# Three partition sums as pairs of fp32r products, with one sum and one denominator moved, in an adaLN block

## The chip, the cores and the metric

The kernel runs on one core of a Trainium2 chip. The metric is the device time of one execution in microseconds, as the median of several runs.

## The reference

A block with adaptive layer norm: linear attention, then a bilinear gated feed-forward layer. The input x has 2048 tokens of 512 numbers, there are 32 heads of 16, and the feed-forward layer is 1376 wide. Everything is fp32.

```python
mod = (silu(c) @ w_mod).reshape(1, 6, 1, 512)
sa, ca, ga, sb, cb, gb = the six rows of mod
h = layernorm(x) * (1 + ca) + sa
q, k, v = heads of h @ wqkv
pq, pk = phi(q), phi(k)            # phi(t) = (t + 1 where t > 0, else exp(t)) + 1e-6
kv = einsum("bhsd,bhse->bhde", pk, v)
z = einsum("bhsd->bhd", pk)        # sum of phi(k) over all tokens
num = einsum("bhqd,bhde->bhqe", pq, kv)
den = einsum("bhqd,bhd->bhq", pq, z)[..., None] + 1e-6
x = x + ga * ((num / den) @ wo)
h = layernorm(x) * (1 + cb) + sb
out = x + gb * (((h @ w_gate) * (h @ w_up)) @ w_down)
```

## The kernel before

The order of all instructions is written out by hand: each engine runs its queue in the order of the code, and waits only for the data it needs. Tiles have 128 partitions and mostly 512 columns. The tokens are 16 tiles in 4 chunks; SBUF tiles come from one pool of 99 buffers, PSUM banks from two pools of four (`acc_bank`, `bank`).

Products are made from split operands: `split` (L182 to L184) copies a tile to fp32r on ScalarE (the high part h, L183) and subtracts it from the original on VectorE, or on another engine named by `low` (the low part l, L184). `product` (L192 to L198) then adds three fp32r products for each pair of tiles: high by high, high by low, low by high.

Sums over the 128 partitions are not split before the change. Row v of mod is gathered in an accumulator tile by `mod_acc` (L156 to L161, VectorE: each w_mod tile times silu(c), added). For the rows that are needed as columns, `mod_col` (L163) multiplies the accumulator by one column of `ones`. For rows 2 (ga) and 5 (gb) `mod_row` (L174 to L179) multiplies a 128x128 tile of ones by the accumulator in one fp32 product of 512 columns (L176), so that each partition holds the sum, and ScalarE copies it out (L178). The sum z of phi(k) is treated likewise: `z_add` (L304) adds the tiles on VectorE into `zacc`, one fp32 product sums over the partitions (L512), and ScalarE writes `zb` (L514).

The main loop (L458 to L517) runs over the 16 tiles i. In tile i TensorE makes the k or q product for two tiles ahead (`proj`, L196 to L198) and adds tile i into the four accumulators of x-hat by phi(k) (`t_tile`, L323 to L325). ScalarE and VectorE make phi (L287, L288, L291), and the dictionary `extra` (L443) hangs the loading and gathering of mod, and the splitting of wo, on tiles 4 to 15. In tile 14 stand the last gathering step of row 5 (L161) and the four splits of wo; in tile 15 the sum of z, `t_tile`, and then row 5's sum.

Behind the loop, VectorE makes `den_z` (L528, L529), which needs zb, and the denominators of the first chunk: `den_a` for a tile is a product with zb (L534) and a sum over each head (L540). ScalarE scales the four accumulators by ca (L583), VectorE adds zb times sa (L584), and both split the four results into `tt` (L183, L184). TensorE has `proj(6)` and `proj(7)` in the meantime, and then the key-value product `kvps` (L592 to L594): 48 products of 128 columns, from wv and `tt`. VectorE then takes the diagonal blocks of it (L601), `w_out` multiplies them into wo and by ga (L571), and the attention output, the second norm and the feed-forward layer follow, with gb scaling w_down (L706, L1043).

Of the kernel before, what the change touches and what calls it, by code (L numbers as in the profile page):

```python
# [9 lines left out]
F32R = mybir.dt.float32r  # L10
# [4 lines left out]
P = 128  # L15
# [7 lines left out]
def tile_adaln_block(  # L23
# [12 lines left out]
    nc = tc.nc  # L36
# [23 lines left out]
    consts = pool("consts", 1)  # L60
# [10 lines left out]
    def T(p, tag, shape=(P, D), dt=F32, bufs=None):  # L71
        cnt[0] += 1
        return p.tile(list(shape), dt, tag="t" if p is tiles else tag, name=f"{tag}_{cnt[0]}", bufs=bufs)

    def B(tag, shape=(P, D), dt=F32):

        return T(tiles, tag, shape, dt)
# [4 lines left out]
    def bank():  # L82
        return T(ps_w, "bank")
# [6 lines left out]
    ones = consts.tile([P, P], F32, name="ones")  # L90
# [17 lines left out]
    def load(src, tag):  # L108
        raw = B(tag, (P, *src.shape[1:]))[:src.shape[0]]
        nc.sync.dma_start(raw, src)  # L110
        return raw
# [4 lines left out]
    def load_mod(v):  # L116
        return [load(wm_v[:, k, v * D:(v + 1) * D], "raw") for k in range(KD)]
# [38 lines left out]
    def mod_acc(acc, raws, ks):  # L156
        for k in ks:
            if k == 0:
                nc.vector.tensor_scalar(acc, raws[k], sc[:, 0:1], None, op0=ALU.mult)
            else:  # L160
                nc.vector.scalar_tensor_tensor(acc, raws[k], sc[:, k:k + 1], acc, op0=ALU.mult, op1=ALU.add)  # L161

    def mod_col(acc, ps):  # L163

        for b in range(KD):
            nc.tensor.matmul(ps[:, b:b + 1], acc[:, b * P:(b + 1) * P], ones[:, 0:1], start=True, stop=True)
        return ps

    def col_out(v, ps, add):
        t = consts.tile([P, KD], F32, name=f"col{v}")  # L170
        nc.vector.tensor_scalar(t, ps[:, :KD], add, None, op0=ALU.add)
        return t

    def mod_row(v, acc):  # L174
        ps = bank()
        nc.tensor.matmul(ps, ones, acc, start=True, stop=True)  # L176
        t = consts.tile([P, D], F32, name=f"row{v}")
        nc.scalar.activation(t, ps, AF.Copy)  # L178
        return t  # L179


    def split(src, h, l, low=None):  # L182
        nc.scalar.activation(h, src, AF.Copy)  # L183
        (low or nc.vector).tensor_tensor(l, src, f32(h), op=ALU.subtract)  # L184

    def split_raw(raw, shape=(P, D), low=None):
        h = B("w", shape, F32R)
        l = B("w", shape, F32R)
        split(raw, h[:raw.shape[0]], l[:raw.shape[0]], low)
        return h, l  # L190
# [82 lines left out]
    NT = NCH * NJ  # L273
# [4 lines left out]
    def proj(i, w, of=bank):  # L278

        ch, j = divmod(i, NJ)  # L280
        ps = of()
        product(ps, [(cut(norm[ch].t[k], j * P, (j + 1) * P), w[k]) for k in range(KD)])
        return ps
# [9 lines left out]
    def k_split_x(i):  # L293
        ch, j = divmod(i, NJ)
        kx[i] = [B("xh", dt=F32R), B("xl", dt=F32R)]
        split(norm[ch].n[j], *kx[i])

    def k_phi(i, ps):
        phi = B("phi")
        phi_a(ps, phi)  # L300
        phi_b(ps, phi)
        phk[i] = phi

    def z_add(i):  # L304
        if i == 1:
            nc.vector.tensor_tensor(zacc, phk[0], phk[1], op=ALU.add)
        elif i > 1:
            nc.vector.tensor_tensor(zacc, zacc, phk[i], op=ALU.add)
        phk.pop(i - 1, None)

    def k_split(i):
        h, l = B("kh", dt=F32R), B("kl", dt=F32R)
        phi = phk[i]
        nc.scalar.activation(h, phi, AF.Identity, bias=eps_phi)
        nc.vector.scalar_tensor_tensor(l, phi, EPS_PHI, f32(h), op0=ALU.add, op1=ALU.subtract)
        kx[i] += [h, l]

    def t_tile(i, *ks):
        xh, xl, kh, kl = kx[i]
        first, last = i == 0, i == NT - 1  # L320
        for k in ks:
            a, b = k * P, (k + 1) * P
            nc.tensor.matmul(tacc[k], xh[:, a:b], kh, start=first, stop=False)  # L323
            nc.tensor.matmul(tacc[k], xl[:, a:b], kh, start=False, stop=False)  # L324
            nc.tensor.matmul(tacc[k], xh[:, a:b], kl, start=False, stop=last)  # L325

    def q_a(i, ps):
        phq[i] = B("h")
        q_ps[i] = ps
        phi_a(ps, phq[i])  # L330

    def q_b(i):
        phi_b(q_ps.pop(i), phq[i])

    zacc = B("z")
# [94 lines left out]
    rows, cols = {}, {}  # L430
    accs = {}

    raw_m, raw_o, wo_s = {}, [], []

    def mod_load(*vs):
        raw_m.update({v: load_mod(v) for v in vs})

    def mod_part(v, *ks):
        if 0 in ks:
            accs[v] = B("f")  # L440
        mod_acc(accs[v], raw_m[v], ks)
# [4 lines left out]
             7: lambda: (wv.extend(split_raw(r) for r in raw_v[3:4]),),  # L446
             8: lambda: (mod_part(2, 0, 1), mod_load(3)),
             9: lambda: (mod_part(2, 2, 3), mod_load(4)),
             10: lambda: (mod_part(3, 0, 1, 2), mod_load(5)),
             11: lambda: (mod_part(3, 3), mod_part(4, 0, 1), rows.update({2: mod_row(2, accs[2])})),  # L450
             12: lambda: (raw_o.extend(load(wo_v[k], "raw") for k in range(KD)), mod_part(4, 2, 3), cols.update({3: col_out(3, mod_col(accs[3], bank()), 0.0)})),
             13: lambda: (mod_part(5, 0, 1, 2), cols.update({4: col_out(4, mod_col(accs[4], bank()), 1.0)})),
             14: lambda: (mod_part(5, 3), wo_s.extend(split_raw(x) for x in raw_o)), 15: lambda: rows.update({5: mod_row(5, accs[5])})}
    q_at = {3: 0, 4: 1, 6: 2, 7: 3}
    ahead = {2: k_ps[2], 3: k_ps[3]}
    turn_at = {4 * ch + j: (ch + 1, 2 * j, 2 * j + 1) for ch in range(1, NCH - 1) for j in range(2)}
    turn_at.update({1: (1, 0, 1), 2: (1, 2, 3)})
    for i in range(NT):  # L458
        ch, j = divmod(i, NJ)
        done = 0  # L460
        if i > 2:
            ahead[i + 2] = proj(i + 2, wk) if i + 2 < NT else proj(i + 6 - NT, wq)
        if i in q_at:
            qps = proj(q_at[i], wq)
        def turn_x():
            to, *ks = turn_at[i]
            nx.transpose(*ks)
            nx.modulated(ca, sa, *ks, cast=nc.vector)
            norm[to:] = [nx]

        fresh = i > 0 and ch + 1 < NCH and j == 0
        if i == 2:
            turn_x()
            wq.extend(split_raw(r) for r in raw_q)
        if fresh:
            nx.xhat(2)
        if 0 < i < NT - 1:
            k_split_x(i + 1)
        if fresh:
            nx.xhat(3)  # L480
        if 0 < i < NT - 1:
            k_split(i + 1)
        if i in turn_at and i != 2:
            t_tile(i, 0, 1)
            done = 2
            turn_x()
        if i == 2:
            t_tile(i, *range(KD))
            done = KD
            ahead[i + 2] = proj(i + 2, wk)  # L490
        if ch + 2 < NCH and j == 2:
            nx2 = Norm(xts[ch + 2])
            nx2.stats(0, 1)
        if ch + 2 < NCH and j == 3:
            nx = nx2
            nx.stats(2, 3)
            nx.rstd_of()
            nx.nmr_of()
            nx.xhat(0, 1)
        if i + 2 < NT:  # L500
            k_phi(i + 2, ahead.pop(i + 2))
        else:
            q_a(i + 6 - NT, ahead.pop(i + 2))
            q_b(i + 6 - NT)
        if i in q_at:
            q_a(q_at[i], qps)
            q_b(q_at[i])
        if i + 1 < NT:
            z_add(i + 1)
        if i == NT - 1:  # L510
            zps = bank()
            nc.tensor.matmul(zps, ones, zacc, start=True, stop=True)  # L512
            zb = consts.tile([P, D], F32, name="zb")
            nc.scalar.activation(zb, zps, AF.Identity, bias=eps_z)  # L514
        t_tile(i, *range(done, KD))
        if i in extra:
            extra[i]()  # L517
    ga, gb, sb, cb = rows[2], rows[5], cols[3], cols[4]


    dens = {}
# [4 lines left out]
    def den_z():  # L526

        nc.vector.reduce_sum(den0, zb.rearrange("p (h i) -> p h i", i=DH), axis=AX.X)  # L528
        nc.vector.tensor_scalar(den0, den0, EPS_PHI, EPS_DEN, op0=ALU.mult, op1=ALU.add)  # L529

    def den_p(ch, *js, on=None):
        for j in js:
            pzs[ch, j] = B("f")
            (on or nc.gpsimd).tensor_tensor(pzs[ch, j], phq[ch * NJ + j], zb, op=ALU.mult)  # L534
# [7 lines left out]
    def den_a(ch, *js, on=None):  # L542

        for j in js:
            den_p(ch, j, on=on)
            den_r(ch, j)
# [13 lines left out]
    def q_tile(i):  # L560
        q_a(i, proj(i, wq))
# [13 lines left out]
            split(f, *wp[-1])  # L575

    den_z()
    den_a(0, 0, 1, on=nc.vector)
    ps = proj(6, wq)
    fs, tt = [], []  # L580
    for k in range(KD):
# [6 lines left out]
        split(f, *tt[-1])  # L588
    q_a(6, ps)
    q_tile(7)  # L590
    kvps = bank()
    for g in range(KD):  # L592
        a, b = g * P, (g + 1) * P
        product(kvps[:, a:b], [(cut(wv[k], a, b), cut(tt[k], a, b)) for k in range(KD)])  # L594
    q_b(6)
    q_b(7)
    den_a(0, 2, on=nc.vector)
    ps = proj(8, wq)
    kvp = (B("xh", dt=F32R), B("xl", dt=F32R))
    kvf = B("n")  # L600
# [7 lines left out]
    ps = proj(9, wq)  # L608
# [470 lines left out]
    ps = proj(11, wq)  # L1079
# [185 lines left out]
```

## Time and profile before

| | |
|---|---|
| median of 3 runs | 566.05 us (565.7 to 566.51) |
| the profiled execution | 565.84 us, its span 564.1 us |
| granted TensorE clock | 0.999 |
| TensorE busy | 556.8 us (99% of the span) |
| VectorE busy | 377.4 us (67%) |
| ScalarE busy | 278.5 us (49%) |
| GpSimd busy | 187.0 us (33%) |

The span is the time from the first to the last instruction in the profile; the execution's own time is 1.7 us longer. In the rows, PE is TensorE, PEld its weight loads, DVE VectorE, ACT ScalarE, POOL GpSimd and SP the queue that issues the DMAs. A row of the timeline gives the start, the time from the start of the first to the end of the last of a few like instructions, engine, line, operation, output and inputs, shapes, and how many they are; in brackets stands how long the engine was idle before, and what released it. Starts of an engine's neighbouring instructions lie closer together than their durations, because the end of one overlaps the start of the next.

### The profile page before, as it was taken

What the parts mean: (1) busy time and instruction counts of PE and PEld (TensorE: products, weight loads), DVE (VectorE), ACT (ScalarE), POOL (GpSimd) and SP (SyncE); (2) the same over time, 40 slices, a digit from 0 to 9 for tenths busy, and PEclk for the clock granted to TensorE, in tenths of its full rate; (3) what the DMA queues carried; (4) which work ended last, traced back from release to release, by engine and by line L of the source; (5) the groups of instructions that cost most, each with busy time, mean ns of one, the idle gap of its engine ahead of it and who ended that gap; (6) DMA issues with size and microseconds to landing.
All of it is one profiled execution on the core that took longest, in us unless ns stands there. A gap on an engine that the chain in (4) does not pass through costs nothing.

```text
span 564.1 us, 7356 instructions
## 1 busy us (share of the span) xinstructions
PE 556.8 (99%) x2568; PEld 457.1 (81%) x2568; DVE 377.4 (67%) x622; ACT 278.5 (49%) x499; POOL 187.0 (33%) x192
## 2 busy tenths in 40 slices
PE   7999999999999999999999999999999999999997
PEld 6788888888888778878878888887888888888886
DVE  7996968868869876759768877756444444344445
ACT  3695866446556546355875454534333333334120
POOL 2000000000011300000598756555667446446200
PEclk9999999999999999999999999999999999999999
DMA  8900224202301001804408363599336022200004
GB/s 286 380 5 2 74 76 131 94 0 72 83 2 57 19 1 38 260 0 150 131 2 295 116 206 112 184 350 310 113 112 189 17 57 56 57 19 2 0 1 149
DMA packets 50309, 59.34 MB, mean 105 GB/s; under 512 B 6432, under 2 KB 27168, under 8 KB 50272
## 3 DMA queue, kind: packets, MB, share of 16 engines
q1 hardware_dynamic: 50272, 58.87, 32.8%
q8 instruction: 20, 0.33, 0.2%
q14 instruction: 17, 0.14, 0.1%
HBM read 43.12 MB, written 15.73 MB: 104 GB/s over the span
## 4 chain that ended last, share of the span: by engine, by line
PE 92%; ACT 2%; DVE 2%; POOL 1%; issue 1%; DMA 1%; SPq 0%; POOLq 0%
PE bank L892 28%; PE acc L972 6%; PE acc L973 6%; PE acc L974 6%; PE acc L662 6%; PE bank L196 5%; PE bank L198 5%; PE bank L197 5%; PE acc L325 3%; PE acc L323 3%; PE acc L324 3%; PE bank L741 2%; PE bank L739 2%; PE bank L740 2%; PE bank L246 2%; PE bank L626 1%
## 5 line engine op out<-in xcount | busy, mean ns | idle before, releaser
L892 PE MATMUL bank<-h,w 128*128 128x512 f32 (+1 forms) x798 | 184.6, 390 | 0.0
L892 PEld LDWEIGHTS bank<-h,w 128*128 128x128 f32 (+1 forms) x798 | 148.4, 186 | 32.4
L897 ACT ACTIVATE bank<-bank 128x512 f32<-128x512 f32 (+1 forms) x38 | 22.1, 582 | 142.9 <-PE bank L892 142.9
L726 DVE TENSOR_TENSOR x<-acc,x 128x512 f32<-128x512 f32 (+1 forms) x73 | 48.9, 683 | 47.5 <-PE acc L974 46.7
L878 POOL TENSOR_TENSOR w<-raw,w 128x256 fp32r<-128x256 f32 (+3 forms) x38 | 42.4, 1115 | 103.0 <-ACT w L871 76.1
L184 POOL TENSOR_TENSOR w<-raw,w 128x512 fp32r<-128x512 f32 (+1 forms) x25 | 34.9, 1401 | 116.0 <-DVE mv L216 87.5
L972 PE MATMUL acc<-w,kh 128*128 128x512 f32 (+2 forms) x154 | 59.6, 387 | 0.0
L973 PE MATMUL acc<-w,kh 128*128 128x512 f32 (+2 forms) x154 | 59.6, 387 | 0.0
L974 PE MATMUL acc<-w,kl 128*128 128x512 f32 (+2 forms) x154 | 59.5, 386 | 0.0
L224 POOL TENSOR_TENSOR rstd<-ve,half 128x4 f32<-128x4 f32 (+1 forms) x10 | 10.6, 1061 | 123.2 <-DVE ve L223 121.6
L184 DVE TENSOR_TENSOR kl<-u,kh 128x512 fp32r<-128x512 f32 (+1 forms) x38 | 27.4, 761 | 31.8 <-ACT kh L183 28.0
L878 POOL TENSOR_TENSOR w<-t,w 128x512 fp32r<-128x512 f32 (+1 forms) x38 | 48.4, 1296 | 0.0
L196 PE MATMUL bank<-w,h 128*128 128x512 f32 x104 | 41.7, 401 | 0.0
L198 PE MATMUL bank<-w,h 128*128 128x512 f32 x104 | 40.6, 390 | 0.0
L197 PE MATMUL bank<-w,h 128*128 128x512 f32 x104 | 40.5, 389 | 0.0
L662 PE MATMUL acc<-w,xh 128*128 128x512 f32 x120 | 38.1, 399 | 0.0
L972 PEld LDWEIGHTS acc<-w,kh 128*128 128x128 f32 (+1 forms) x154 | 28.9, 188 | 6.0
L974 PEld LDWEIGHTS acc<-w,kl 128*128 128x128 f32 (+1 forms) x154 | 28.9, 188 | 5.9
L973 PEld LDWEIGHTS acc<-w,kh 128*128 128x128 f32 (+1 forms) x154 | 28.9, 188 | 5.9
L951 DVE TENSOR_TENSOR u<-bank,u 128x512 f32<-128x512 f32 (+1 forms) x19 | 13.1, 692 | 30.3 <-PE bank L892 26.8
L233 ACT ACTIVATE n<-x,nmr,rstd 128x512 f32<-128x512 f32 x30 | 22.7, 804 | 16.0 <-DVE nmr L227 16.0
L183 ACT ACTIVATE w<-raw 128x512 fp32r<-128x512 f32 (+2 forms) x44 | 26.2, 619 | 2.8 <-DMA raw<-in_A_wqkv_dram 1.9
(188 smaller groups left out, 1108.8 us busy)
## 6 DMA issues: line engine op xcount, KB each, us to landing
raw<-in_w_mod_dram SPq DMA_DIRECT2D x24, 256.0 KB, 3.8
raw<-in_B_w_down_dram SPq DMA_DIRECT2D x20, 256.0 KB, 3.4
raw<-in_B_w_gate_dram SPq DMA_DIRECT2D x36, 128.0 KB, 3.9
raw<-in_B_w_up_dram SPq DMA_DIRECT2D x36, 128.0 KB, 3.9
x<-in_A_x_dram SPq DMA_DIRECT2D x16, 256.0 KB, 5.8
kept<-f SPq DMA_DIRECT2D x16, 256.0 KB, 2.0
f<-kept SPq DMA_DIRECT2D x16, 256.0 KB, 4.3
side_s<-h SPq DMA_DIRECT2D x16, 256.0 KB, 2.5
```

Source lines behind the costliest of these rows:

```text
L183: nc.scalar.activation(h, src, AF.Copy)
L184: (low or nc.vector).tensor_tensor(l, src, f32(h), op=ALU.subtract)
L196: nc.tensor.matmul(ps, ah, bh, start=i == 0, stop=False)
L197: nc.tensor.matmul(ps, ah, bl, start=False, stop=False)
L198: nc.tensor.matmul(ps, al, bh, start=False, stop=i == n - 1)
L662: nc.tensor.matmul(yps[i], x, y, start=False, stop=k == KD - 1 and x is al, skip_group_check=True)
L726: nc.vector.tensor_tensor(xt[:, a:b], dn[j][:, a:b], xt[:, a:b], op=ALU.add)
L878: sub = lambda out, x, y: (on or nc.gpsimd).tensor_tensor(out, x, f32(y), op=ALU.subtract)
L892: mm = lambda x, y, **kw: nc.tensor.matmul(ps, x[:, k], y, skip_group_check=True, **kw)
L972: nc.tensor.matmul(ps, hh[:, a:b], dh[:n, c:d], start=i == 0, stop=False)
L973: nc.tensor.matmul(ps, hh[:, a:b], dl[:n, c:d], start=False, stop=False)
L974: nc.tensor.matmul(ps, hl[:, a:b], dh[:n, c:d], start=False, stop=i == len(hs) - 1)
```

## The change

A copy `ones_r` of the tile of ones in fp32r is made on VectorE at the start. `row_sum` takes a split pair and adds two fp32r products with it, for the high and the low part. Row 2, row 5 and z are split first: by ScalarE (high part) and GpSimd (low part). Row 2's accumulator is split in tile 10, one tile ahead of its sum; z and row 5's accumulator in tile 14, z in front of the four splits of wo on ScalarE, row 5 behind them. Row 5's sum no longer stands at the end of tile 15 but behind `proj(7)`, directly in front of the key-value product, and its copy out is behind the phi of tile 7 on ScalarE. Of the three denominators of the first chunk that stand in front of the key-value product's operands or right behind their phi, tile 1's moves from the first place to the second.

```diff
+    ones_r = consts.tile([P, P], F32R, name="ones_r")
+    nc.vector.tensor_copy(ones_r, ones)
+
+    def row_sum(pair):
         ps = bank()
-        nc.tensor.matmul(ps, ones, acc, start=True, stop=True)
+        for n, x in enumerate(pair):
+            nc.tensor.matmul(ps, ones_r, x, start=n == 0, stop=n == 1)
+        return ps
+
+    def mod_row(v, pair):
+        ps = row_sum(pair)
         t = consts.tile([P, D], F32, name=f"row{v}")
         nc.scalar.activation(t, ps, AF.Copy)
         return t
...
-             10: lambda: (mod_part(3, 0, 1, 2), mod_load(5)),
-             11: lambda: (mod_part(3, 3), mod_part(4, 0, 1), rows.update({2: mod_row(2, accs[2])})),
+             10: lambda: (pairs.update({2: split_raw(accs[2], low=nc.gpsimd)}), mod_part(3, 0, 1, 2), mod_load(5)),
+             11: lambda: (mod_part(3, 3), mod_part(4, 0, 1), rows.update({2: mod_row(2, pairs[2])})),
...
-             14: lambda: (mod_part(5, 3), wo_s.extend(split_raw(x) for x in raw_o)), 15: lambda: rows.update({5: mod_row(5, accs[5])})}
+             14: lambda: (mod_part(5, 3), wo_s.extend(split_raw(x) for x in raw_o), pairs.update({5: split_raw(accs[5], low=nc.gpsimd)}))}
+    pairs = {}
...
+        if i == NT - 2:
+            pairs["z"] = split_raw(zacc, low=nc.gpsimd)
         if i == NT - 1:
-            zps = bank()
-            nc.tensor.matmul(zps, ones, zacc, start=True, stop=True)
+            zps = row_sum(pairs["z"])
...
-    den_a(0, 0, 1, on=nc.vector)
+    den_a(0, 0, on=nc.vector)
...
     q_tile(7)
+    gb = mod_row(5, pairs[5])
     kvps = bank()
...
-    den_a(0, 2, on=nc.vector)
+    den_a(0, 1, 2, on=nc.vector)
```

More of the change, by code (lines that the diff above doesn't have):

```diff
@@ L172, in col_out @@
         return t
-    def mod_row(v, acc):
+    ones_r = consts.tile([P, P], F32R, name="ones_r")
+    nc.vector.tensor_copy(ones_r, ones)
+    def row_sum(pair):
         ps = bank()
-        nc.tensor.matmul(ps, ones, acc, start=True, stop=True)
+        for n, x in enumerate(pair):
[3 more added lines that the diff above has]
+        ps = row_sum(pair)
         t = consts.tile([P, D], F32, name=f"row{v}")
@@ L517, in tile_adaln_block @@
             extra[i]()
-    ga, gb, sb, cb = rows[2], rows[5], cols[3], cols[4]
+    ga, sb, cb = rows[2], cols[3], cols[4]
     dens = {}
```

## The prediction

> **What bounds the kernel now.** I read the page first, then what TensorE waits for, then the timeline of each engine around 97 to 145 us, where all changed lines stand. Busy shares, the chain that ended last by engine, and TensorE's largest waits after the start of the kernel:
>
> ```profile
> PE 556.8 (99%) x2568; PEld 457.1 (81%) x2568; DVE 377.4 (67%) x622; ACT 278.5 (49%) x499; POOL 187.0 (33%) x192
> PE 92%; ACT 2%; DVE 2%; POOL 1%; issue 1%; DMA 1%; SPq 0%; POOLq 0%
> PE acc L246 <- ACT n L233: 0.4, 1, 0.4
> PE acc L386 <- DVE h L266: 0.4, 1, 0.4
> ```
>
> TensorE is busy nearly throughout. So a microsecond taken from its queue is a microsecond of the end, unless another engine then comes too late for it. That is the whole question.
>
> **Three fp32 sums become pairs of fp32r products.** TensorE's timeline around two of them (start, duration, line, tiles; durations overlap, so I go by starts):
>
> ```profile
> 126.34 1.02 PE L512 MATMUL bank<-z,ones 128*128 128x512 f32 x2
> 126.80 0.79 PE L323 MATMUL acc<-kh,xh 128*128 128x512 f32 x1
> 127.43 0.39 PE L324 MATMUL acc<-kh,xl 128*128 128x512 f32 x1
> ...
> 129.96 1.02 PE L176 MATMUL bank<-f,ones 128*128 128x512 f32 x2
> 131.05 0.39 PE L197 MATMUL bank<-w,h 128*128 128x512 f32 x1
> ...
> 136.30 0.22 PE L196 MATMUL bank<-w,w 128*128 128x128 f32 x1
> ```
>
> From 131.05 to 136.30 stand 23 fp32r products of 512 columns: 5.25 / 23 = 0.228 each. From L512's start to L324's are 1.09 us, one such product among them: the fp32 sum takes 1.09 - 0.228 = 0.862; L176 gives the same (131.05 - 129.96 - 0.228). Two fp32r products take 0.456, so each sum saves 0.406, and three save **1.22 us**. The weights are again one 128x128 tile a product, as in the neighbours; I add nothing for them. The Trainium skill ("FP8 and Floating Point Precision", TensorE Precision Notes) counts four passes for a true fp32 product; four of 0.228 would be 0.91, and the estimate by that page a saving of 1.37. The 0.862 is measured here, and I keep it.
>
> **The copy of ones.** One more VectorE instruction in front of the first statistics:
>
> ```profile
> 1.50 0.45 DVE L138 CAST w<-f 128x512 fp32r<-128x512 f32 x1
> 3.98 0.70 DVE L215 BATCH_NORM_STATS2 st<-x 128x6 f32<-128x512 f32 x1 [2.04 <-DMA x<-in_A_x_dram]
> ```
>
> It costs at most the 0.45 of a cast four times as wide and lies in 2.04 us of waiting for x: nothing. Without that cover it would cost 0.45.
>
> **The halves of row 2's sum** are made one tile earlier: a ScalarE copy behind phi, and a GpSimd subtraction. TensorE's row of that sum, and the next pauses of ScalarE and VectorE:
>
> ```profile
> 104.50 1.02 PE L176 MATMUL bank<-f,ones 128*128 128x512 f32 x2
> ...
> 99.03 0.63 ACT L183 ACTIVATE xh<-n 128x512 fp32r<-128x512 f32 x1 [1.23 <-PE acc L324]
> ...
> 109.61 0.69 DVE L291 SCALAR_TENSOR_TENSOR phi<-bank,phi 128x512 f32<-128x512 f32 x1 [1.60 <-ACT phi L288]
> ```
>
> The copy (0.63) fits into 1.23 us of waiting. GpSimd can push VectorE back by part of one subtraction (its price comes next), which 1.60 us of pause take up before TensorE asks for anything. The row's product stands at 104.5, five microseconds after: nothing. If the pauses were gone, some 0.6 us of VectorE delay would be left.
>
> **What GpSimd's subtractions do to VectorE.** The first row below says that GpSimd did nothing for 87.5 us before 165.17, so the new cost isn't shown in place. Later rows show both at work on SBUF (GpSimd, then VectorE at the same times, and L549 undisturbed):
>
> ```profile
> 165.17 2.54 POOL L184 TENSOR_TENSOR w<-raw,w 128x512 fp32r<-128x512 f32 x2 [87.52 <-DVE mv L216]
> 176.98 1.28 POOL L184 TENSOR_TENSOR w<-raw,w 128x512 fp32r<-128x512 f32 x1 [5.28 <-ACT w L183]
> 185.00 2.99 POOL L184 TENSOR_TENSOR w<-raw,w 128x512 fp32r<-128x512 f32 x2 [6.74 <-ACT w L183]
> ...
> 177.13 1.28 DVE L549 TENSOR_TENSOR den<-den,den 128x128 f32<-128x128 f32 x1
> 185.91 0.93 DVE L557 SCALAR_TENSOR_TENSOR h<-h,den 128x512 f32<-128x512 f32 x1
> 186.77 1.78 DVE L706 TENSOR_TENSOR raw<-raw,row 128x512 f32<-128x512 f32 x1
> 212.26 0.28 DVE L549 TENSOR_TENSOR den<-den,den 128x128 f32<-128x128 f32 x1
> ```
>
> L549 takes 1.28 in place of 0.28: it stands still until GpSimd is done. L557 and L706 against the two GpSimd subtractions from 185.00 to 187.99 show turns: GpSimd 1.28, one VectorE instruction, GpSimd again, and L706 ends 0.56 after it (186.77 + 1.78 = 188.55). So each subtraction costs 1.28 and holds back any VectorE instruction with two SBUF inputs that comes after it. The rule of the Trainium skill that speaks against this change says the same ("SBUF — State Buffer", Who interferes with whom): VectorE with two SBUF inputs contends with a GpSimd instruction that reads SBUF, and who issues first keeps the pair to its end. What that does in this place, by rows of ScalarE and VectorE:
>
> ```profile
> 122.27 2.18 ACT L183 ACTIVATE w<-raw 128x512 fp32r<-128x512 f32 x4
> ...
> 123.01 0.68 DVE L308 TENSOR_TENSOR z<-z,phi 128x512 f32<-128x512 f32 x1
> 123.61 0.75 DVE L161 SCALAR_TENSOR_TENSOR f<-raw,sc,f 128x512 f32<-128x512 f32 x1
> 124.27 2.49 DVE L184 TENSOR_TENSOR w<-raw,w 128x512 fp32r<-128x512 f32 x4
> 127.83 0.69 DVE L291 SCALAR_TENSOR_TENSOR h<-bank,h 128x512 f32<-128x512 f32 x1 [1.08 <-ACT h L288]
> 130.57 0.68 DVE L534 TENSOR_TENSOR f<-h,zb 128x512 f32<-128x512 f32 x1
> 132.23 2.74 DVE L584 SCALAR_TENSOR_TENSOR n<-zb,col,n 128x512 f32<-128x512 f32 x4 [0.26 <-ACT n L583]
> 134.89 2.49 DVE L184 TENSOR_TENSOR w<-n,w 128x512 fp32r<-128x512 f32 x4
> 141.93 0.69 DVE L601 TENSOR_TENSOR n<-bank,mask 128x512 f32<-128x512 f32 x1 [1.57 <-PE bank L198]
> ```
>
> All here comes 0.41 earlier by row 2's saving. The last add into z ends at 123.01 + 0.68 - 0.41 = 123.28. Behind it ScalarE's queue now holds z's copy (123.3 to 123.9), the four copies of wo (one each 0.52) and the copy of row 5's accumulator (ends 126.5). GpSimd subtracts for z from 124.0 to 125.3. TensorE reaches z's first product at 125.93 and the one that needs GpSimd at 126.16: 0.9 us to spare. But VectorE's first subtraction for wo, ready at 124.5, is held until 125.3 and ends at 125.85; two more follow to 127.05; GpSimd, asking at 126.6, goes next to 128.3; the fourth ends at 128.85. L291, in the queue behind it, starts at 128.75 where it would have started at 127.42.
>
> From L291 to the end of the first denominator are 130.57 - 127.83 = 2.74: L584 can start at 131.49. The second denominator, 1.3 us that stood here (130.57 to 131.9), is now behind q_b; both last ones then end near 140.5, and L601, which already waits 1.57 us for the key-value product, can't start before 141.2. From L584's start to the last low part are 134.89 + 2.49 - 132.23 = 5.15: it is there at **136.64**. ScalarE has row 5's output no longer in front of L583, so the four L583 are no later than L584 wants; its two copies more delay phi by some 0.3, and zb is still there before VectorE asks.
>
> **What TensorE finds at the key-value product:**
>
> ```profile
> 137.26 0.28 PE L196 MATMUL bank<-w,w 128*128 128x128 f32 x1
> 137.44 0.33 PE L197 MATMUL bank<-w,w 128*128 128x128 f32 x1
> 137.60 0.28 PE L198 MATMUL bank<-w,w 128*128 128x128 f32 x1
> ```
>
> Steps of 0.18 and 0.16 where 0.11 is usual: it already waits 0.12 for the fourth low part (134.89 + 2.49 = 137.38). After the change the product starts at 136.30 - 1.22 = 135.08 (row 5's pair stands in front of it, the fp32 sum is gone from before), and asks for the fourth low part 1.07 later, at 136.15. With 136.64, and the 0.05 that a wait takes to pass, it stands 0.54; some 0.04 more until it is in step. So 0.58 of waiting in place of 0.12.
>
> **Sum:** -1.22 - 0.12 + 0.58 = **-0.76 us**. Bounds: no waiting at all -1.34; waiting 0.5 longer than worked out (errors of 0.1 in each of five joints) -0.3. Against the profiled execution, 565.84, this gives 565.1; that execution is 0.2 under the median 566.05, from which it gives 565.3. I say 565.2. Loads are not moved in the queue; their buffers shift by a few, which lets the four loads of wo go at some 102 to 106 us as before and be used at 123.
>
> ```profile
> 102.16 3.85 SPq L110 DMA_DIRECT2D raw<-in_A_wo_dram  x4
> ```
>
> **Rivals.** First, VectorE is not late: GpSimd's second subtraction slips behind the fourth of VectorE, or the copies stand earlier than I place them. Then the wait at the key-value product is gone: -1.34, 564.7. For it: both are decided by some 0.3 us. Against: L706 waited its turn in just such a case. Second, TensorE's time isn't worth its price, since a chain through the other engines sets the end further on (the 0.4 us wait at L246): no change, 566.05. Against it stands that this chain hangs on TensorE itself. Third, slower: GpSimd's subtraction for z loses its turn. If z's copy came over 0.5 us later than worked out, VectorE's four subtractions would be in front, and if they keep the turn, GpSimd starts at 126.9 and ends at 128.2, where TensorE wants it at 126.16: 2.04 us of standing still, net 2.04 - 1.34 = +0.7, 566.75. Against it: the copy waits only for the add, and the turns alternate.
>
> **Chances.** Runs of one kernel spread over 0.8 us here, and 0.2% (1.13 us) is about what a measurement can tell from no change. Forecast 0.45, of which 0.10 end over 1.13 faster; first rival 0.37 (0.34); second 0.06; third 0.12, of which 0.08 over 1.13 slower with the spread. So faster 0.44, same 0.48, slower 0.08. The range goes from the first rival less 0.3 of spread, 564.4, to no change and a little, 566.2; the third rival is left out.
>
> **What would show it.** In the new profile: pairs of ones_r products 0.23 apart; GpSimd from 124.0 and again from about 127; a VectorE L184 of 1.3 us or more on the wo tiles, and its L291 near 128.7; TensorE waiting 0.5 us inside the key-value product and nowhere before. No such wait means the first rival; a wait at the z products means the third. A time above 566.2 or under 564.4 would show my sum to be wrong.

## The result and the profile after

The changed kernel takes 565.27 us (median of 22 runs, 564.90 to 566.34), the kernel before 566.05 us on the same chip (22 runs, 565.68 to 566.51). The ratio is 0.9986, interval 0.9980 to 0.9992: faster by 0.78 us, which is 0.14%. 565.2 had been predicted, range 564.4 to 566.2; the change stays under the 0.2% that was set as its bound for telling faster from no change, and only the 22 runs of each tell it.

The profiled execution of the changed kernel took 565.39 us, its span is 563.7. From its page, the busy shares and the chain that ended last by engine:

```profile
PE 555.7 (99%) x2568; PEld 457.0 (81%) x2568; DVE 379.7 (67%) x623; ACT 280.3 (50%) x502; POOL 191.6 (34%) x195
PE 89%; DVE 3%; issue 3%; ACT 2%; POOL 1%; DMA 1%; SPq 1%; POOLq 0%; DVEq 0%
```

The same number of products, 1.1 us less of them, and three instructions more on GpSimd and on ScalarE. All rows from here on have the line numbers of the changed kernel (some lie a line or two off in an experiment). L180 is the pair of products of a sum. L191 copies a high part and L192 subtracts a low part (L183 and L184 before), and L204 to L206 are the three products (L196 to L198 before). On VectorE, L299 makes phi (L291 before), L316 adds into z (L308 before), and L594 adds zb times sa to the operands of the key-value product (L584 before).

Where the time went is read from TensorE's timeline of the changed kernel (start, duration, line, tiles). Its fourth row here, at 135.47, is the first product behind row 5's pair, which is the first of the key-value product; the last row is the first product of the projection that follows:

```profile
104.82 0.64 PE L180 MATMUL bank<-w,ones_r 128*128 128x512 f32 x2
105.30 0.40 PE L204 MATMUL bank<-w,h 128*128 128x512 f32 x1
...
134.99 0.64 PE L180 MATMUL bank<-w,ones_r 128*128 128x512 f32 x2
135.47 0.22 PE L204 MATMUL bank<-w,w 128*128 128x128 f32 x1
...
136.09 0.27 PE L204 MATMUL bank<-w,w 128*128 128x128 f32 x1
136.37 0.33 PE L205 MATMUL bank<-w,w 128*128 128x128 f32 x1
136.53 0.27 PE L206 MATMUL bank<-w,w 128*128 128x128 f32 x1
136.64 0.28 PE L204 MATMUL bank<-w,w 128*128 128x128 f32 x1
136.97 0.33 PE L205 MATMUL bank<-w,w 128*128 128x128 f32 x1
...
141.26 0.45 PE L204 MATMUL bank<-w,h 128*128 128x512 f32 x1
```

- A pair takes 0.48 from its first start to the next product's (105.30 - 104.82, and 135.47 - 134.99), against 0.862 for the fp32 sum: 0.38 saved each, 1.15 in all.
- Steps of 0.28, 0.16, 0.33 and 0.16, where 0.11 is usual, are the waits for the third and the fourth low part. From 135.47 to 141.26 the product takes 5.79. A kernel without any wait there (the one with wo earlier, in the experiments) takes 5.31, the kernel before 5.43 (136.30 to 141.73). So TensorE waits 0.48 in place of 0.12.
- -1.15 - 0.12 + 0.48 = **-0.79**, against -0.78 of the medians. In these two profiles the key-value product ends only 0.47 earlier (141.73 and 141.26), because this execution of the changed kernel comes to row 2's sum 0.32 later (104.82 against 104.50, behind a start-up wait of 1.6 in place of 1.0): 0.79 less 0.32.

Who makes TensorE wait stands in the timelines of GpSimd and VectorE (in brackets the idle time before, and what ended it):

```profile
124.38 1.30 POOL L192 TENSOR_TENSOR w<-z,w 128x512 fp32r<-128x512 f32 x1 [23.62 <-ACT w L191]
126.98 1.60 POOL L192 TENSOR_TENSOR w<-f,w 128x512 fp32r<-128x512 f32 x1 [1.31 <-ACT w L191]
```

```profile
124.85 4.28 DVE L192 TENSOR_TENSOR w<-raw,w 128x512 fp32r<-128x512 f32 x4 [0.56 <-ACT w L191]
129.06 0.68 DVE L299 SCALAR_TENSOR_TENSOR h<-bank,h 128x512 f32<-128x512 f32 x1
131.77 2.73 DVE L594 SCALAR_TENSOR_TENSOR n<-zb,col,n 128x512 f32<-128x512 f32 x4
134.42 2.49 DVE L192 TENSOR_TENSOR w<-n,w 128x512 fp32r<-128x512 f32 x4
```

VectorE's four subtractions for wo take 4.28 in place of 2.49, since both GpSimd subtractions fall into them: taken singly, the first of the four takes 1.37 and the last 1.78, the two between 0.68 each. L299 comes at 129.06, and the last low part at 134.42 + 2.49 = 136.91. The groups behind L299 follow without a pause, so whatever L299 loses the key-value product waits for.

### The profile page after: what moved, and what is told of

The parts are those of the page before. It is cut to its first block, busy times and chain, and to the rows that moved or that the text cites. A ratio compares the mean times of both kernels' runs of the same rounds, so it can differ in the third digit from the quotient of the medians.

```text
span 563.7 us, 7369 instructions
## 1 busy us (share of the span) xinstructions
PE 555.7 (99%) x2568; PEld 457.0 (81%) x2568; DVE 379.7 (67%) x623; ACT 280.3 (50%) x502; POOL 191.6 (34%) x195
## 4 chain that ended last, share of the span: by engine, by line
PE 89%; DVE 3%; issue 3%; ACT 2%; POOL 1%; DMA 1%; SPq 1%; POOLq 0%; DVEq 0%
PE bank L903 29%; PE acc L984 6%; PE acc L983 6%; PE acc L985 6%; PE acc L673 6%; PE bank L204 4%; PE bank L205 4%; PE bank L206 4%; PE acc L333 2%; PE acc L331 2%; PE acc L332 2%; PE bank L752 2%; PE bank L750 2%; PE bank L751 2%; PE bank L254 2%
## 5 line engine op out<-in xcount | busy, mean ns | idle before, releaser
L192 POOL TENSOR_TENSOR w<-raw,w 128x512 fp32r<-128x512 f32 (+1 forms) x25 | 35.1, 1408 | 64.5 <-ACT w L191 64.5
L192 DVE TENSOR_TENSOR kl<-u,kh 128x512 fp32r<-128x512 f32 (+1 forms) x38 | 27.3, 760 | 31.8 <-ACT kh L191 28.0
L204 PE MATMUL bank<-w,h 128*128 128x512 f32 x104 | 40.9, 393 | 0.0
L206 PE MATMUL bank<-w,h 128*128 128x512 f32 x104 | 40.6, 390 | 0.0
L191 ACT ACTIVATE w<-raw 128x512 fp32r<-128x512 f32 (+2 forms) x44 | 26.2, 619 | 3.3 <-DMA raw<-in_A_wqkv_dram 2.3
```

Source lines behind the costliest of these rows:

```text
L204: nc.tensor.matmul(ps, ah, bh, start=i == 0, stop=False)
L206: nc.tensor.matmul(ps, al, bh, start=False, stop=i == n - 1)
```

## The experiments

Each changes the changed kernel, unless said otherwise. The "wait" is what the steps of the key-value product add up to over their usual size (0.06 for the first, 0.11 each behind it, 5.31 in all); where the clock falls later in the product, only the steps ahead of the fall are counted. The kernel before ran beside them with medians of 566.12 (the four of the first group: all low parts on VectorE, denominators as before, wo one tile earlier, z's subtraction twice) and 566.18 (the other four). The two groups ran on two chips, so the ratio is the safer figure between them.

| kernel | wait, us | median, us | ratio and interval |
|---|---|---|---|
| all low parts on VectorE | 0.08 | 565.10 | 0.9981 [0.9973, 0.9990] |
| denominators as before | 1.81 | 571.56 | 1.0083 [1.0058, 1.0107] |
| wo one tile earlier | 0 | **564.72** | 0.9974 [0.9965, 0.9983] |
| z's GpSimd subtraction twice | 1.60 | 570.43 | 1.0057 [1.0036, 1.0079] |
| row 5 back at tile 15's end | 0.43 | 565.45 | 0.9986 [0.9977, 0.9994] |
| wo earlier, sums in fp32 | 0 | 565.99 | 0.9998 [0.9989, 1.0006] |
| wo earlier, denominators as before | 0.56 | 565.28 | 0.9984 [0.9975, 0.9992] |
| one 0.7 us instruction more ahead | 1.22 | 566.46 | 1.0025 [1.0002, 1.0047] |

**Is it GpSimd's hold on VectorE that TensorE waits for?** The low parts of all three sums go to VectorE, in its own queue (the three calls are put side by side here).

```
-  split_raw(accs[2], low=nc.gpsimd)   split_raw(accs[5], low=nc.gpsimd)   split_raw(zacc, low=nc.gpsimd)
+  split_raw(accs[2])                  split_raw(accs[5])                  split_raw(zacc)
```

> The changed kernel with all three low parts on VectorE in place of GpSimd, ScalarE's queue unchanged. Theory (GpSimd's two subtractions in tile 14 hold VectorE's subtractions of wo, and that makes the key-value product's operands late): VectorE gets 0.6 us more for each low part but is held no more; its phi behind them starts near 128.3 in place of 129.06, TensorE's wait inside the key-value product falls from 0.48 to about 0.1, total about 564.9. Rival (the copies that the change puts into ScalarE's queue make VectorE late, GpSimd is innocent): the wait stays at 0.5 or grows by the added VectorE work to 1 or more, total 565.3 to 566.

Measured 565.10 (564.66 to 565.26), 1.0 under the kernel before. VectorE's timeline of this kernel:

```profile
124.12 0.69 DVE L192 TENSOR_TENSOR w<-z,w 128x512 fp32r<-128x512 f32 x1 [0.70 <-ACT w L191]
124.73 0.75 DVE L161 SCALAR_TENSOR_TENSOR f<-raw,sc,f 128x512 f32<-128x512 f32 x1
125.39 2.49 DVE L192 TENSOR_TENSOR w<-raw,w 128x512 fp32r<-128x512 f32 x4
127.80 0.68 DVE L192 TENSOR_TENSOR w<-f,w 128x512 fp32r<-128x512 f32 x1
128.40 0.68 DVE L299 SCALAR_TENSOR_TENSOR h<-bank,h 128x512 f32<-128x512 f32 x1
```

VectorE does two subtractions more, at 0.6 each, and still comes to L299 0.66 earlier than with GpSimd's help (0.21 of it is this execution's earlier start: its last add into z stands at 122.74, that of the changed kernel at 122.95): wo takes 2.49 again. One step of 0.16 is left of the wait. So the wait of the changed kernel is GpSimd's hold, and "help" of 1.3 us from GpSimd costs VectorE more than the 0.6 that it spares. Its key-value product ends where that of the kernel with wo earlier does (140.65 and 140.59), yet the median is 0.4 higher. In the two profiles TensorE of this kernel falls behind the other in small pieces over the rest of the run, from 0.06 at that place to 0.49 at the last product; what delays it there isn't settled. The granted clock (the share of its full clock that TensorE gets, 1.00 at full) stands at 0.95 in this profile almost from start to end, though its products of 512 columns start 0.227 apart as elsewhere, so a mean clock on record doesn't prove a loss by itself.

**Is it the place of the wo subtractions?** They move one tile earlier, so that GpSimd's two subtractions meet none of them.

```
-  13: lambda: (mod_part(5, 0, 1, 2), cols.update(...)),
-  14: lambda: (mod_part(5, 3), wo_s.extend(split_raw(x) for x in raw_o), pairs.update({5: ...}))}
+  13: lambda: (mod_part(5, 0, 1, 2), cols.update(...), wo_s.extend(split_raw(x) for x in raw_o)),
+  14: lambda: (mod_part(5, 3), pairs.update({5: ...}))}
```

> The changed kernel with the four splits of wo in tile 13 in place of tile 14, GpSimd's work unchanged. Theory: nothing of VectorE's with two SBUF inputs is left to be held but what has time; phi starts near 127.5, the wait inside the key-value product is gone, total 1.2 to 1.3 us under the old kernel: 564.8. Rival (any GpSimd subtraction near the sums costs, wherever VectorE's work stands): the wait stays, 565.3.

Measured 564.72 (564.27 to 565.01): faster than both kernels. Timelines of GpSimd and of VectorE:

```profile
124.65 1.30 POOL L192 TENSOR_TENSOR w<-z,w 128x512 fp32r<-128x512 f32 x1 [24.08 <-ACT w L191]
125.90 1.30 POOL L192 TENSOR_TENSOR w<-f,w 128x512 fp32r<-128x512 f32 x1
```

```profile
127.60 0.69 DVE L299 SCALAR_TENSOR_TENSOR h<-bank,h 128x512 f32<-128x512 f32 x1 [3.03 <-ACT h L296]
130.34 2.73 DVE L594 SCALAR_TENSOR_TENSOR n<-zb,col,n 128x512 f32<-128x512 f32 x4
132.99 2.49 DVE L192 TENSOR_TENSOR w<-n,w 128x512 fp32r<-128x512 f32 x4
```

The same GpSimd work runs with VectorE idle: L299 has a pause of 3.03 ahead of it and stands at 127.60. The last low part is there at 135.48, TensorE starts the product at 135.28, and nothing waits. -1.15 - 0.12 = -1.27 would give 564.8 from the result's median before; the kernel before that ran beside it took 566.12, so it is 1.40 faster.

**What are the products worth without the moves?** The kernel with wo earlier again, with each sum as one fp32 product of the whole tile, nothing of them split (the last line puts the three places side by side).

```
-  for n, x in enumerate(pair):
-      nc.tensor.matmul(ps, ones_r, x, start=n == 0, stop=n == 1)
+  nc.tensor.matmul(ps, ones, pair, start=True, stop=True)
...
-  split_raw(accs[2], low=nc.gpsimd)   split_raw(accs[5], low=nc.gpsimd)   split_raw(zacc, low=nc.gpsimd)
+  accs[2]                             accs[5]                             zacc
```

> The kernel with the splits of wo in tile 13, but the three sums as single fp32 products again and nothing of them split, everything else in its new place. Theory (the gain is TensorE's time for the sums, 0.38 each, and the old wait of 0.12): 1.15 us over the kernel with wo in tile 13, so 565.9, and 0.1 to 0.2 under the old kernel. Rival (the gain comes from the new order on ScalarE and VectorE): it stays near 564.8.

Measured 565.99 (565.50 to 566.77). TensorE's timeline has the fp32 products at 1.02 again, here row 5's:

```profile
135.92 1.02 PE L179 MATMUL bank<-f,ones 128*128 128x512 f32 x2
```

So all moves together (row 5's place, one denominator behind, wo earlier) are worth 0.0 to 0.2 with fp32 sums, which fits the 0.12 of waiting that they take away; the remaining 565.99 - 564.72 = 1.27 is the products' (1.15 by their starts; 1.21 if each kernel is taken against the kernel before that ran beside it).

**What does row 5's place do?** Back at the end of tile 15, as before the change.

```
+  gb = mod_row(5, pairs[5])          # at the end of the loop over tiles
   ga, sb, cb = rows[2], cols[3], cols[4]
...
-  gb = mod_row(5, pairs[5])          # in front of the key-value product
   kvps = bank()
```

> The changed kernel with row 5's pair of products and its copy back at the end of tile 15, as in the old order. Theory (only VectorE's chain to the last low part and TensorE's total before the key-value product matter): TensorE asks for the operands at the same time and they come at the same time, since ScalarE's copy of row 5 in front of L593 lies before VectorE wants it; no change, 565.3. Rival (the move of row 5 is worth what it takes off ScalarE in front of the operands): 0.5 us more wait, 565.8.

Measured 565.45 (564.70 to 567.15): the same as the changed kernel, with a wait of 0.43. ScalarE's timeline:

```profile
131.02 0.60 ACT L186 ACTIVATE row<-bank 128x512 f32<-128x512 f32 x1 [1.60 <-PE bank L180]
131.51 2.42 ACT L594 ACTIVATE n<-acc,col 128x512 f32<-128x512 f32 x4
```

ScalarE had idled 1.60 before the row's output. VectorE comes to the scaled accumulators only at 132.56, without a pause in front:

```profile
132.56 2.73 DVE L595 SCALAR_TENSOR_TENSOR n<-zb,col,n 128x512 f32<-128x512 f32 x4
```

The first of ScalarE's four (L594 in this kernel) had ended at 132.20, so the row's output holds no one up. This part of the change was worth nothing here.

**And the moved denominator?** Undone alone, and undone on the kernel with wo earlier.

```
   den_z()
-  den_a(0, 0, on=nc.vector)
+  den_a(0, 0, 1, on=nc.vector)
...
-  den_a(0, 1, 2, on=nc.vector)
+  den_a(0, 2, on=nc.vector)
```

> The changed kernel with the second denominator back in its old place, in front of the key-value product's operands. Theory (VectorE's chain from phi to the last low part is what TensorE waits for): all of the denominator's 1.3 us is added to the wait of 0.48, total about 566.6, slower than the old kernel. Rival (the wait hangs on ScalarE's copies or on TensorE itself): no change, 565.3.

> The kernel with the splits of wo in tile 13 and the second denominator in its old place in front of the operands. Theory (VectorE's chain has some 0.9 us to spare once GpSimd holds it no more, and the denominator takes 1.3): a wait of 0.5 inside the key-value product, total about 565.2, no halved clock. Rival (a denominator in that place costs the whole 1.3 or sets off the halved clock as without the move of wo): 566 or over 570.

On the kernel with wo earlier: 565.28 (564.78 to 565.87), a wait of 0.56, and 564.72 + 0.56 = 565.28. Undone alone: the profiled execution took 566.61, the other five 571.27 to 571.87. TensorE's timeline and VectorE's in the profiled one:

```profile
135.38 0.22 PE L204 MATMUL bank<-w,w 128*128 128x128 f32 x1
136.40 0.33 PE L205 MATMUL bank<-w,w 128*128 128x128 f32 x1 [0.79 <-DVE w L192]
```

```profile
133.01 2.73 DVE L594 SCALAR_TENSOR_TENSOR n<-zb,col,n 128x512 f32<-128x512 f32 x4
```

L594 comes 1.24 later than in the changed kernel, and the wait is 1.81 in place of 0.48: 565.27 + 1.33 = 566.60, and the 566.61 agrees. The five others lost 5 us more, at a mean granted clock of 0.99 in place of 1.0. No expectation had this loss: the theory gave 566.6, which only the profiled execution met.

**A longer wait, made in two other ways.** GpSimd subtracts for z a second time, into a tile that nobody reads; and, separately, VectorE makes the first reduction of the denominator twice.

```
   pairs["z"] = split_raw(zacc, low=nc.gpsimd)
+  again = B("w", dt=F32R)
+  nc.gpsimd.tensor_tensor(again, zacc, f32(pairs["z"][0]), op=ALU.subtract)
```

> The changed kernel with z's low part computed twice on GpSimd, the second time into a tile that nobody reads. Theory (turns at SBUF between GpSimd and VectorE): VectorE loses one more turn of 1.25 us, the wait inside the key-value product grows from 0.48 to about 1.7, total about 566.5. Rival (GpSimd only delays its own later work): row 5's low part comes 1.3 us later and is still in time, no change, 565.3.

```
   nc.vector.reduce_sum(den0, zb.rearrange("p (h i) -> p h i", i=DH), axis=AX.X)
+  nc.vector.reduce_sum(den0, zb.rearrange("p (h i) -> p h i", i=DH), axis=AX.X)
```

> The changed kernel with one more VectorE sum of 0.7 us (the first of den_z made twice) in front of the operands. Theory on the wait: it grows from 0.48 to about 1.2, total about 566.0. On the clock: with 1.6 and 1.8 us of wait most executions lose 5 us more at a half clock; if a threshold lies between 0.5 and 1.6, this one shows on which side 1.2 is: all executions near 566.0, or some near 571.

With the second subtraction, GpSimd's and VectorE's timelines:

```profile
125.54 1.75 POOL L522 TENSOR_TENSOR w<-z,w 128x512 fp32r<-128x512 f32 x1
127.26 1.75 POOL L192 TENSOR_TENSOR w<-f,w 128x512 fp32r<-128x512 f32 x1
```

```profile
124.77 5.38 DVE L192 TENSOR_TENSOR w<-raw,w 128x512 fp32r<-128x512 f32 x4 [0.56 <-ACT w L191]
130.08 0.68 DVE L299 SCALAR_TENSOR_TENSOR h<-bank,h 128x512 f32<-128x512 f32 x1
```

One GpSimd subtraction more, 1.10 more for wo. GpSimd's second and third now take 1.75 each, their own 1.3 and most of a VectorE subtraction of 0.6 ahead of them, so the two engines take turns. That is the hold, dose for dose. The time fell into two groups, as above: four of 12 executions took 566.40 to 567.21 (the wait alone gives 565.27 + 1.60 - 0.48 = 566.39), eight 569.60 to 572.01. With the reduction made twice, seven of 12 took 565.66 to 566.66 (median 566.18; the wait alone gives 566.01) and five 569.55 to 571.39; the longest of 35 runs of the kernel before beside them took 567.81. Here both profiles caught the long kind. Stretches of the first of the two (stretch, its length, then busy time and count of TensorE, its weight loads, VectorE, ScalarE and GpSimd, the granted clock with 1.00 as full, DMA share, GB/s):

```profile
138.00:139.00 1.00, 1.00 (x9) 1.00 (x10) 1.00 (x2) 0.98 (x2) 0.00 (x0) 1.00 1.05 304
139.00:140.00 1.00, 1.00 (x7) 1.00 (x6) 0.96 (x3) 0.00 (x0) 0.00 (x0) 0.52 0.92 262
140.00:142.00 2.00, 2.00 (x11) 2.00 (x11) 1.82 (x3) 0.00 (x0) 0.00 (x0) 0.50 1.06 322
...
146.00:148.00 2.00, 2.00 (x6) 1.52 (x6) 1.90 (x4) 0.63 (x1) 0.00 (x0) 0.50 0.00 0
148.00:150.00 2.00, 2.00 (x8) 1.58 (x7) 1.39 (x3) 0.00 (x0) 0.00 (x0) 0.68 0.00 0
150.00:152.00 2.00, 2.00 (x11) 1.63 (x10) 0.58 (x1) 1.23 (x2) 0.00 (x0) 1.00 0.00 0
```

and of the second, behind the beginning of its key-value product in TensorE's timeline:

```profile
137.57 0.22 PE L204 MATMUL bank<-w,w 128*128 128x128 f32 x1
137.98 0.33 PE L205 MATMUL bank<-w,w 128*128 128x128 f32 x1 [0.19 <-DVE w L192]
```

```profile
14.00:28.00 14.00, 13.12 (x53) 9.98 (x53) 11.14 (x26) 6.83 (x11) 1.07 (x1) 0.88 1.04 372
...
140.00:142.00 2.00, 2.00 (x18) 2.00 (x18) 1.97 (x4) 0.77 (x2) 0.00 (x0) 0.91 1.01 269
142.00:144.00 2.00, 2.00 (x12) 2.00 (x11) 1.62 (x3) 0.00 (x0) 0.00 (x0) 0.50 1.07 330
...
148.00:150.00 2.00, 2.00 (x9) 1.56 (x9) 1.93 (x4) 0.00 (x0) 0.00 (x0) 0.88 0.00 0
```

The granted clock falls to 0.50 one or two us after the last of the waits and stays there for 10 us in the first (139.04 to 149.28 in the trace's clock record) and 7 in the second (141.65 to 148.48), which costs half of that: 5.1 and 3.4 us. (The second lost some 1.7 more in its start-up, at 0.88 over 14 us.) TensorE is busy all the time in every row from 138 on: the half clock doesn't show in its busy share, only in the count of products and in the clock's column.

## Why the prediction was right, point by point

**The mechanism** stands. VectorE is held on the wo tiles by both GpSimd subtractions, by turns. L299 comes at 129.06; less the 0.32 by which this execution runs later, that is 128.74, where 128.75 was worked out. Taking the hold away in two ways took the wait away; adding one subtraction added to it.

**Two terms were mis-sized, and their errors cancel.** "Two fp32r products take 0.456": they measure 0.48, so the three sums save 1.15, not 1.22. Why a pair that stands alone takes 0.02 more than two products in a row of their like wasn't tried. "So 0.58 of waiting": it was 0.48. The last low part came at 136.91 - 0.32 = 136.59 (136.64 predicted), while TensorE came to the product at 135.47 - 0.32 = 135.15, later by the 0.07 that three pairs took more than 135.08. The sum of -0.76 was -0.79. That they cancel is no luck: VectorE's last low part sets the end, so the 0.07 by which TensorE comes later is 0.07 that it waits less. Most of the rest is the low part itself, there 0.05 earlier than predicted.

**Nothing for the halves of row 2's sum:** right, though GpSimd did hold VectorE there. Timelines of GpSimd and of VectorE in the changed kernel:

```profile
99.15 1.61 POOL L192 TENSOR_TENSOR w<-f,w 128x512 fp32r<-128x512 f32 x1 [21.24 <-ACT w L191]
```

```profile
99.52 0.68 DVE L299 SCALAR_TENSOR_TENSOR phi<-bank,phi 128x512 f32<-128x512 f32 x1
100.12 1.18 DVE L316 TENSOR_TENSOR z<-z,phi 128x512 f32<-128x512 f32 x1
109.56 0.69 DVE L299 SCALAR_TENSOR_TENSOR phi<-bank,phi 128x512 f32<-128x512 f32 x1 [0.82 <-ACT phi L296]
```

GpSimd works until 100.76. L299, which has one of its inputs in PSUM (`bank`), takes its usual 0.68 beside it; the add into z, with both inputs in SBUF, takes 1.18 for its usual 0.68. The pause behind shrinks from 1.60 to 0.82 and still isn't zero. The Trainium skill ("SBUF — State Buffer", Who interferes with whom) has the held instruction wait for the other to end; the trace agrees, with the addition that in a row of such instructions the turns alternate.

**The first rival** (VectorE not late, 564.7) is not what the changed kernel does, but its sum is right: the kernel with wo earlier makes that case and takes 564.72, 1.40 under the kernel before beside it, where 1.34 was worked out. **The second** (a chain through other engines sets the end) falls: the wait at the transposes is the same as before, and the saving is still there at the last products of the run, 560.26 before and 559.80 after.

```profile
294.03 0.76 PE L254 MATMUL acc<-ident,n 128*128 128x128 f32 x5 [0.38 <-ACT n L241]
559.80 0.28 PE L985 MATMUL acc<-w,kl 128*128 128x256 f32 x1
```

**The third** (z's low part loses its turn) did not happen: GpSimd began at 124.38 and TensorE has no wait at z's products. But its price may have been too low. It counted a wait of 2.04 us as 2.04, and the runs show that waits of 1.22 to 1.81 inside the key-value product often cost some 3 to 5 us more; one at z's products was not run. The same holds for the bound "waiting 0.5 longer than worked out": 1.08 of waiting lies between 0.56, where no execution lost its clock there, and 1.22, where 5 of 12 did. So the range held with at most 0.7 us of VectorE's time to spare.

**The second denominator** behind q_b was read only as VectorE time that moves out of the way. That is what it is (0.56 on the kernel with wo earlier, 1.33 of waiting on the changed one), but without it the changed kernel would have been slower than the kernel before by 0.8%, ratio 1.0083 [1.0058, 1.0107]. The prediction did not price that.

## What to carry to other kernels

In this kernel, giving a vector instruction to GpSimd relieved VectorE only where VectorE had no work with two SBUF inputs of its own at that time: lay it beside a pause, or move VectorE's work, before counting the gain (here a move of one line was worth 0.55 us by the medians, and the wait of 0.48 was gone). Price a multi-pass product by the distance of starts, pair by pair, and look at what comes just behind in the same queue: a saving of 1.2 us on TensorE was worth 0.8 because VectorE was then late by half a microsecond. And where TensorE waits several times within a few microseconds, read the granted clock of the following ten.

## What the runs showed of the hardware that was not expected

Waits of 1.22, 1.60 and 1.81 us in sum within some 2.4, 2.8 and 3.0 us, in pieces of which the longest is 0.35 us in the first case (a step of 0.41 where 0.06 is usual) and 0.96 in the last, are followed by the half clock in 5 of 12, 8 of 12 and, by their times and mean clocks, 5 of 6 executions. Behind waits of 0.56 and less no profile has it, and the times of 22 runs of the changed kernel and 42 of the four others whose waits are so short and whose sums are pairs show none, with one case open: the longest, 567.15 at a mean clock of 0.996 (row 5 back at tile 15's end), has no profile. The profiled execution of the same kernel, 566.12 at 0.997, has its half clock in the start-up, from 16.10 to 19.51. The Trainium skill ("TensorE: Matmul & The Clock Gate", Why this matters for your kernels) asks for no idle gaps over some 3 us; by that rule none of these kernels should have lost its clock, so the measurement decides against it as a bound. The same page of the Trainium skill (What's actually happening) has a window of 3.4 us that runs on its own, which would fit a share of executions rather than all. The traces agree with such a window: the half clock lasts 10.24 and 6.83 us behind the waits, and 3.41 in the start-up of two profiles (16.10 to 19.51, and 18.77 to 22.18), which is three, two and one times 3.413. From the first rise to the full clock (5.92 and 5.12 in the two profiles) to the two falls are 133.12 and 136.53 us, 39 and 40 times as much.

The sum of the waits in one such step does not decide by itself. In the step that ends with the fall it was 1.4 us (135.63 to 139.04) and 0.8 (138.24 to 141.65). The profiled execution of the kernel with the denominators as before kept its clock through 1.5 us between 134.33 and 137.75, where its steps lie if they are counted from its own first rise at 8.04. That step begins with 1.05 us of products of 512 columns, and the two others hold products of 128 columns alone. A step full of those without a wait kept its clock too (136.69 to 140.10, counted from 6.98, in the kernel with wo earlier). Too little work of TensorE in one step would fit all four; no run here was made to test that.
